# Nine small blank products for one large, and five pieces of work put in another place, in a fused attention and mixer kernel

## The chip, the cores and the metric

The kernel runs on one core of a Trainium2 chip. A core has a matrix engine (TensorE, in the profile PE, with its weight loads as PEld), a vector engine (VectorE, DVE), a scalar engine (ScalarE, ACT), a general engine (GpSimd, POOL) and SyncE (SP), which here only issues transfers. The engines run side by side, each through its own list of instructions in order, and wait for one another through semaphores. Transfers are done by 16 DMA engines; SP, and in this kernel ScalarE too, issue them. The metric is the device time of one execution in microseconds (us).

## The reference

Linear attention with decay by blocks of 64 positions, and then a mixer with a low-rank product and a two-layer part. Shapes: q, k, v are (4, 8, 768, 64), all fp32.

```
per block b of 64 positions, per head:
  intra = ((qb kb^T) * Dmask) vb          # Dmask[i,j] = lam^(i-j) for i >= j
  inter = (qb * lam_pow) kv_state
  out   = intra + inter
  kv_state = lam^64 * kv_state + (kb * rev_pow)^T vb
x = out as (4, 768, 512)
u = x + ((x^T U) V)^T                     # U: 768 x 32, V: 32 x 768
result = u + relu(u w_ch1) w_ch2          # w_ch1: 512 x 2048, w_ch2: 2048 x 512
```

U, V and both weights come as 64-bit floats, so the kernel turns their words into fp32 on VectorE and ScalarE. Products of the mixer are done to near fp32 precision: each operand is split into a high part, a low part and a sum of both, and three products are added up.

## The kernel before, in words

**Attention.** A step s covers 128 positions of one batch; there are 24 steps, six to a batch. The order of all instructions of this stage is written out by hand in the list `pieces` (L698 to L732): the loop over s appends names, and each name is one function. In a step the order around the change is: `prep(s+1)` transposes q and k of the next step on PE and copies them to SBUF on ScalarE; then `intra(s)` multiplies the masked scores `sm` by v into the PSUM tile `px` (L506 to L517), `state(s)` makes the next state kv from k and v (absent in the last step of a batch), `next_v` issues the next load of v from ScalarE, and `inter(s)` multiplies the scaled q by the state and adds that into the same `px` (L519 to L527); then ScalarE copies `px` to `x_nat` (L531). After it come the scores of the next step (`pss`, L463), and VectorE multiplies them by the mask in two halves (`sm`, L472). Up to step 6 `state` stands ahead of `intra`, from step 7 on behind it. `px` has one buffer of two banks, and so have `pss` and `pqk`, the tile for the transposes.

**Start.** While the first loads run, PE multiplies a blank tile with itself (`keep_busy`, L397 to L401): two products, then the tiny product `pl` which spreads lam over the partitions (L830), then three more. The first transposes follow.

**Mixer, first product.** The last steps of attention leave work that runs between the products of the first four pairs (`hidden`, L875 to L906): the list `rest` puts the low-rank part and the transposes (`turn`) of the last steps at given places between the matmuls. Each pair adds up in PSUM banks tagged a1 and a2, two buffers each; ScalarE copies the first (`r`, L896), VectorE adds the second (L905). A transposed step of the last two groups goes through a bank tagged b1, from where ScalarE copies it to the tile `u_whole` (L664). Steps 16 and 17 are turned within the first pair's products.

Then single products (L958, 145 us to 295 us of the profile), and products by seven forms (`seven_of`), which save one product in eight. Between them, `strew` puts side work at the ticks of a counter.

**Mixer, second product.** Each of 96 steps needs a block of the first product's result, fetched from memory (`rm`), its relu and its split into three parts: one ScalarE instruction (L1296) and two on VectorE (L1297, L1298) in `split`. The first two splits are strewn over the last four ticks of the products by forms, where VectorE also adds up the forms' results (`add_to`, L1199), which read the PSUM banks that the next products write. The steps that follow (L1312, L1314, L1316) are laid out in the same loop that fetches and splits ahead.

Of the kernel before, what the change touches and what calls it, by code (L numbers as in the profile page):

```python
# [11 lines left out]
AF = mybir.ActivationFunctionType  # L12
ALU = mybir.AluOpType

P = 128
# [3 lines left out]
def kernel(  # L19
# [28 lines left out]
    nc = tc.nc  # L48

    B, H, S, D = q.shape  # L50
    HP = H // 2
    NT = S // P
# [7 lines left out]
    NS = B * NT  # L60
# [5 lines left out]
    NEAR = 1.0 - 2.0**-13  # L66
# [19 lines left out]
    ends = []  # L86
# [223 lines left out]
    def two_banks(name, tag):  # L310
        return psf.tile([P, 2, N], FP32, tag=tag, name=name)
# [12 lines left out]
    raw = {}  # L324
# [68 lines left out]
    st = {}  # L393
    kv = {}
    half = [slice(0, D), slice(D, P)]

    def keep_busy(n):  # L397

        out = two_banks("idle", "pm")[:, 0]
        for i in range(n):  # L400
            nc.tensor.matmul(out=out[:, 0:P], lhsT=blank, rhs=blank, start=True, stop=True)  # L401

    qts, kts = {}, {}

# [97 lines left out]
    def next_v(s):  # L502
        del raw[s, "v"]
        load_next("v", nc.scalar)

    def intra(s):  # L506

        st[s]["px"] = both = two_banks("px", "px")
        px = both[:, :, 0 : HP * D].rearrange("p x (a e) -> p x a e", a=HP)
        sm, vr, alone = st[s]["sm"], raw[s, "v"], s % NT == 0  # L510
        for x in range(2):
            for a in range(HP):
                for t in range(2):
                    nc.tensor.matmul(  # L514
                        out=px[half[t], x, a, :], lhsT=sm[:, x, a, half[t]],
                        rhs=vr[:, 2 * a + x, :], start=(a == 0), stop=(alone and a == HP - 1),
                    )  # L517

    def inter(s):  # L519

        px = st[s]["px"][:, :, 0 : HP * D].rearrange("p x (a e) -> p x a e", a=HP)
        for a in range(HP if s % NT else 0):
            for x in range(2):
                for t in range(2):
                    nc.tensor.matmul(  # L525
                        out=px[half[t], x, a, :], lhsT=st[s]["qs"][half[x], a, half[t]],
                        rhs=kv[s][half[x], a, :], start=False, stop=(a == HP - 1),  # L527
                    )
        pool, tag = (att, "x10") if s % 10 == 5 else (x_pool, "x")
        xs[s] = pool.tile([P, C], FP32, tag=tag, name="x_nat")  # L530
        nc.scalar.copy(xs[s].rearrange("p (a x e) -> p x a e", a=HP, x=2), px)  # L531
        del st[s]
# [110 lines left out]
    whole, whole_pool = {}, []  # L643

    def store(s):
        nc.sync.dma_start(out=u_d[s], in_=xs[s])

    def turn(s):

        g, n = divmod(s, TG)  # L650
        if n == 0 and g >= FG:
            whole[g] = whole_pool[0].tile([P, CT, N], FP32, tag="u", name="u_whole")
        elif n == 0:
            uhl[g] = hl_pool.tile([P, 2, CT, N], F32R, tag="hl", name="u_hl")
            ud[g] = d_pool.tile([P, CT, N], F32R, tag="d", name="u_d")
        if g >= FG:
            pt = bank([P, CT, P], "put", "b1")
            for ct in range(CT):
                nc.tensor.transpose(
                    out=pt[:, ct, :], in_=xs[s][:, ct * P : (ct + 1) * P], identity=ident  # L660
                )
            store(s)
            del xs[s]
            nc.scalar.copy(whole[g][:, :, n * P : (n + 1) * P], pt)  # L664
            return

        hi, low, diff = (
            by_halves(what)[:, 2 * n : 2 * n + 2].rearrange("p t c i -> p t (c i)")
            for what in (uhl[g][:, 0], uhl[g][:, 1], ud[g])
        )  # L670
        both = both_halves(s + 1)[:, :, 0 : 2 * P]
        pt = both.rearrange("p t (c i) -> p t c i", i=D)
        for ct in range(CT):
            for n in range(2):
                nc.tensor.transpose(
                    out=pt[:, n, ct, :], in_=xs[s][half[n], ct * P : (ct + 1) * P],
                    identity=ident[half[n], half[n]],
                )
# [14 lines left out]

        splits[s] = split
# [4 lines left out]
    for s in range(NS):  # L699
        b, c = divmod(s, NT)  # L700
        done = s - NT - 1
        more = s + 1 < NS
        turns = done > 0 and (done - 1) // TG < FG
        mixes = 0 <= done < NS - NT - 1
        rows = c == 0 and b > 0
        step = [("fade", s)] * (c > 0)
        step += [("mix", done)] * (mixes and c != 1) + [("turn", done - 1)] * turns
        step += [("split", done - 1)] * turns
        step += [("next_of_low", b - 1)] * (s == NT)
        step += [("prep", s + 1)] * more  # L710
        step += [("mix", done + 1)] * (not more)
        step += [("next_of_low", b - 1)] * (rows and s > NT)
        step += [("scale", s + 1)] * more
        step += [("mixed", done)] * (mixes and c != 1)
        step += [("late", s - 1)] * (1 < s < NT - 1 or s > NT)
        step += [("turned", done - 2)] * (done > 1 and c == 1)
        step += [("mixed", done + 1)] * (not more)
        both = [("intra", s), ("state", s)]
        step += (both if s > NT else both[::-1]) + [("next_v", s), ("inter", s)]
        step += [("next_of_low", b - 1)] * rows  # L720
        step += [("late", s)] * (s < 2 or s in (NT - 1, NT))
        step += [("turned", done - 1)] * (done > 0 and c > 0)
# [17 lines left out]
    run = {  # L740
        "prep": prep, "fade": fade, "scores": scores, "masked": masked, "inter": inter,
        "intra": intra, "state": state,
        "low": low, "low_rows": low_rows, "next_of_low": next_of_low, "mix": mix, "turn": turn,
        "mixed": mixed, "store": store, "next_v": next_v, "split": lambda s: splits.pop(s)(),
# [69 lines left out]
    blank = x_pool.tile([P, C], FP32, tag="x", name="blank")[:, 0:P]  # L814
# [13 lines left out]
    pl = two_banks("pl", "pss")[:, 0, 0:H]  # L828
    keep_busy(2)
    nc.tensor.matmul(out=pl, lhsT=lam_row[:, H:], rhs=lam_row[:, 0:H], start=True, stop=True)  # L830
    keep_busy(3)
    nc.vector.tensor_copy(out=lamb, in_=pl)
    constants()
    powers()
# [96 lines left out]
    for i, (pair, ft) in enumerate(head):  # L931
        before = {}
        for unit, n, *piece in rest:
            if unit == i:
                before.setdefault(n, []).append(piece)
        hidden(ft, pair, before)
        for n, step in side:
            if n == i:
                step()
# [219 lines left out]
    for t in range(4, len(stream_steps)):  # L1159
        n = 2 * t - (4 if t == 4 else 5)  # L1160
# [124 lines left out]
    rs, ms = {}, {}  # L1285
# [6 lines left out]
    def split(i):  # L1292
        r = rs.pop(i)
        ms[i] = m = m_pool.tile([P, 3, N], F32R, tag="m", name="m")
        hi, low = m[:, 0].bitcast(FP32), m[:, 1].bitcast(FP32)
        nc.scalar.activation(out=m[:, 0], in_=r, func=AF.Relu, scale=NEAR)  # L1296
        nc.vector.scalar_tensor_tensor(m[:, 1], r, 0.0, hi, ALU.max, ALU.subtract)  # L1297
        nc.vector.scalar_tensor_tensor(m[:, 2], hi, E, low, ALU.mult, ALU.subtract)  # L1298

    us = {}  # L1300
    acc = {}
# [87 lines left out]
    for n in range(3):  # L1389
        strew((total - 9 + n,), [lambda n=n: fetch(n)])  # L1390
    for n in range(2):
        strew((total - 4 + 2 * n,), [lambda n=n: split(n)])
    w2_late = [w2_split(ft) for ft in range(EARLY, FT)]
    for n in range(2):
        strew((total - 2 + n,), w2_late[n][:1])
# [25 lines left out]
    for i in range(FT - EARLY, len(steps) - STAG):  # L1421
        g, ft = steps[i]
# [11 lines left out]
    for n in range(TG):  # L1434
        ends = [slice(0, C // 2), slice(C // 2, C)] if n == TG - 1 else [slice(0, C)]
# [36 lines left out]
```

## Time and profile before

| what | value |
|---|---|
| median of 3 runs (lowest to highest) | 640.4 us (638.09 to 643.14) |
| the profiled execution: its time, its span | 640.24 us, 638.5 us |
| PE busy | 628.4 us, 98% of the span |
| weight loads, VectorE, ScalarE, GpSimd busy | 83%, 73%, 52%, 23% |
| granted TensorE clock over the span | 1.000 |
| share of PE in the chain that ended last | 95% |
| moved by DMA | 129.61 MB, mean 203 GB/s |

The page of the profile gives busy time of each engine. Its chain follows the work back from the last instruction, at each step to whatever released it. A line of the timeline gives the start, the length, the engine, the line of the kernel, what is written from what, the shape, how many records were merged, and in brackets how long the engine had been idle and what ended that; a line of the chain gives start, length and what ran. "issue" is time in which an engine waited for nothing that the profile can name. The ends of matmuls are modelled, so neighbouring ones overlap in the timeline and do not in the chain.

### The profile page before, as it was taken

The page shows a single profiled execution, that of the slowest core. Times are in us where ns is not written, and L with a number is a line of the kernel's source. Part 1 is how long each engine was busy: PE and PEld are TensorE (multiplying, and loading weights), DVE is VectorE, ACT ScalarE, POOL GpSimd, SP SyncE. Part 2 cuts the span into 40 slices and gives each one's busy share as a digit, 9 for nine tenths or more (in the row PEclk, how much of TensorE's full clock was granted, in tenths as well). Part 3 has the DMA queues.
Part 4 walks back from the last instruction along what each step waited for, and adds up shares of the span by engine and source line. Part 5 has one row for each costly group of instructions (what it writes and reads, how often), then busy time and mean ns, then how long its engine had stood idle before and what let it go on. Part 6 is the DMA issues. An engine that isn't in the chain of part 4 may idle for free.

```text
span 638.5 us, 13622 instructions
## 1 busy us (share of the span) xinstructions
PE 628.4 (98%) x5197; PEld 529.0 (83%) x5197; DVE 463.0 (73%) x740; ACT 334.3 (52%) x615; POOL 147.0 (23%) x125
## 2 busy tenths in 40 slices
PE   8899999999999999999999999999999999999997
PEld 7888989888888888888888878888888888888886
DVE  6756778757888788797888799685674755855844
ACT  4675767445777777778777654232322322323220
POOL 4475959100000000000566500030110300300300
PEclk9999999999999999999999999999999999999999
DMA  9979996347798888855776696362363363532521
GB/s 230 244 186 269 233 248 163 135 175 268 260 354 281 280 306 290 292 195 190 250 232 229 227 332 216 112 225 95 113 216 99 127 203 93 190 131 99 182 83 66
DMA packets 141955, 129.61 MB, mean 203 GB/s; under 512 B 82562, under 2 KB 99970, under 8 KB 141890
## 3 DMA queue, kind: packets, MB, share of 16 engines
q1 hardware_dynamic: 116768, 122.32, 59.4%
q10 hardware_dynamic: 25122, 6.42, 4.5%
q8 instruction: 41, 0.67, 0.4%
q14 instruction: 24, 0.20, 0.1%
HBM read 79.04 MB, written 49.28 MB: 201 GB/s over the span
## 4 chain that ended last, share of the span: by engine, by line
PE 95%; ACT 2%; issue 1%; DMA 1%; DVE 1%; DVEq 0%; ACTq 0%
PE pz L958 24%; PE pz L1314 14%; PE pz L1312 14%; PE pd L1316 13%; PE z L958 4%; PE px L514 4%; PE pss L463 4%; PE p L958 3%; PE pz L889 2%; PE d L958 2%; PE px L525 2%; PE pqk L416 2%; PE c L958 2%; PE pkv L486 1%; PE pd L900 1%
## 5 line engine op out<-in xcount | busy, mean ns | idle before, releaser
L1296 ACT ACTIVATE m<-rm 128x512 fp32r<-128x512 f32 x96 | 60.6, 631 | 174.6 <-PE pd L1316 136.6
L1297 DVE SCALAR_TENSOR_TENSOR m<-rm,m 128x512 fp32r<-128x512 f32 x96 | 71.6, 747 | 82.1 <-ACT m L1296 82.1
L958 PE MATMUL pz<-u_hl,w 128*128 128x512 f32 x448 | 110.3, 389 | 0.0
L1312 PE MATMUL pz<-w_hl,m 128*128 128x512 f32 x264 | 102.7, 389 | 0.0
L1314 PE MATMUL pz<-w_hl,m 128*128 128x512 f32 x264 | 102.7, 389 | 0.0
L1316 PE MATMUL pd<-w_d,m 128*128 128x512 f32 (+1 forms) x267 | 101.4, 387 | 0.0
L958 PEld LDWEIGHTS pz<-u_hl,w 128*128 128x128 f32 x448 | 84.1, 188 | 17.4
L285 POOL TENSOR_TENSOR w<-w 128x512 fp32r<-128x512 f32 x29 | 40.5, 1415 | 211.4 <-DVE w L279 197.1
L1298 DVE SCALAR_TENSOR_TENSOR m<-m 128x512 fp32r<-128x512 f32 x96 | 74.9, 780 | 3.1
L1344 POOL TENSOR_TENSOR o<-o,u 128x512 f32<-128x512 f32 x20 | 29.8, 1519 | 199.1 <-DVE o L1340 199.1
L958 PE MATMUL pz<-u_d,w 128*128 128x512 f32 x224 | 59.9, 389 | 0.0
L1316 PEld LDWEIGHTS pd<-w_d,m 128*128 128x128 f32 x267 | 49.9, 188 | 10.3
L1312 PEld LDWEIGHTS pz<-w_hl,m 128*128 128x128 f32 x264 | 49.6, 188 | 10.3
L1314 PEld LDWEIGHTS pz<-w_hl,m 128*128 128x128 f32 x264 | 49.6, 188 | 10.2
L958 PEld LDWEIGHTS pz<-u_d,w 128*128 128x128 f32 x224 | 42.0, 188 | 8.8
L1312 PE MATMUL pz<-w,m 128*128 128x512 f32 x120 | 46.7, 389 | 0.0
L1316 PE MATMUL pd<-w,m 128*128 128x512 f32 x120 | 46.7, 389 | 0.0
L1314 PE MATMUL pz<-w,m 128*128 128x512 f32 x120 | 46.7, 389 | 0.0
L965 ACT ACTIVATE pz<-pz 128x512 f32<-128x512 f32 x56 | 32.5, 581 | 26.4 <-PE pz L958 26.4
L472 DVE TENSOR_TENSOR sm<-pss,mask 128x512 f32<-128x512 f32 x48 | 30.9, 686 | 19.8 <-PE pss L463 19.8
L969 ACT ACTIVATE r<-pz 128x512 f32<-128x512 f32 x56 | 33.2, 595 | 12.0 <-PE pz L958 11.4
L196 DVE SCALAR_TENSOR_TENSOR sc<-words,sc 128x512 uint32<-128x512 uint32 (+2 forms) x34 | 23.8, 700 | 17.6 <-ACT sc L178 17.6
(140 smaller groups left out, 1119.5 us busy)
## 6 DMA issues: line engine op xcount, KB each, us to landing
r_d<-r SPq DMA_DIRECT2D x96, 256.0 KB, 2.9
rm<-r_d SPq DMA_DIRECT2D x96, 256.0 KB, 2.6
words<-in_moe_w_ch_dram SPq DMA_DIRECT2D x30, 512.0 KB, 5.1
wf<-forms_d SPq DMA_DIRECT2D x56, 128.0 KB, 2.9
u_d<-x_nat SPq DMA_DIRECT2D x24, 256.0 KB, 4.2
u<-u_d SPq DMA_DIRECT2D x24, 256.0 KB, 4.5
qraw<-in_q_dram SPq DMA_DIRECT2D x23, 256.0 KB, 4.6
out_dram<-o SPq DMA_DIRECT2D x23, 256.0 KB, 2.0
```

The source lines that it names most:

```text
L285: engine.tensor_tensor(out=st["third"], in0=st["low"].bitcast(FP32), in1=st["hi"].bitcast(FP32), op=ALU.subtract,)
L472: nc.vector.tensor_tensor(out=sm[:, x], in0=pss[:, x], in1=mask[:, x], op=ALU.mult)
L958: nc.tensor.matmul(out=out, lhsT=weights, rhs=moving, start=start and i == 0, stop=i == len(pieces) - 1, skip_group_check=not start,)
L965: nc.scalar.mul(acc, acc, 1.0 + E)
L969: nc.scalar.mul(r, acc, 4096.0)
L1296: nc.scalar.activation(out=m[:, 0], in_=r, func=AF.Relu, scale=NEAR)
L1297: nc.vector.scalar_tensor_tensor(m[:, 1], r, 0.0, hi, ALU.max, ALU.subtract)
L1298: nc.vector.scalar_tensor_tensor(m[:, 2], hi, E, low, ALU.mult, ALU.subtract)
L1312: nc.tensor.matmul(out=pz, lhsT=m[:, 0, cols], rhs=hi, start=first, stop=False)
L1314: nc.tensor.matmul(out=pz, lhsT=m[:, 1, cols], rhs=low, start=False, stop=end)
L1316: nc.tensor.matmul(out=pd[:, part], lhsT=m[:, 2, cols], rhs=third[:, part], start=first, stop=end, skip_group_check=part.stop != C,)
L1344: nc.gpsimd.tensor_tensor(out=o, in0=o, in1=u, op=ALU.add)
```

## The change

Six edits, all of place or number:

1. `keep_busy` makes its first two products of a call with 128 columns and the rest with 16 columns of the blank tile, and the second call makes 11 products instead of 3. So ahead of the first transposes stand two of 128 and nine of 16 columns.
2. In steps 5, 7 and 23 `inter` comes ahead of `intra`, and so the first to write `px`; the flags that start and end the accumulation are set accordingly. The tile is taken by whichever comes first.
3. The ScalarE copy of `px` becomes a function of its own, `take_x`, behind both; in the other steps it stands where it stood.
4. In `turn` of step 17 the ScalarE copy to `u_whole` is put off until all of the first pair's products are issued, so it stands behind that pair's two `r` copies on ScalarE.
5. `split` is cut in two, and the VectorE half of the second split is strewn one tick later. On VectorE its two instructions thereby move behind three of `add_to`'s.
6. With that, one load of `rm` on SP, whose buffer those instructions empty, comes to stand behind a load of u instead of ahead of it.

Apart from these, the order of instructions on each engine is the same.

```diff
         for i in range(n):
-            nc.tensor.matmul(out=out[:, 0:P], lhsT=blank, rhs=blank, start=True, stop=True)
+            k = P if i < 2 else D // 4
+            nc.tensor.matmul(
+                out=out[0:k, 0:k], lhsT=blank[:, 0:k], rhs=blank[:, 0:k], start=True, stop=True
+            )
...
+    inter_first = (NT - 1, NT + 1, NS - 1)
...
+        begins, ends = s not in inter_first, s in inter_first or s % NT == 0
...
-                        rhs=vr[:, 2 * a + x, :], start=(a == 0), stop=(alone and a == HP - 1),
+                        rhs=vr[:, 2 * a + x, :], start=(begins and a == 0),
+                        stop=(ends and a == HP - 1),
...
-                        rhs=kv[s][half[x], a, :], start=False, stop=(a == HP - 1),
+                        rhs=kv[s][half[x], a, :], start=(begins and a == 0),
+                        stop=(not begins and a == HP - 1),
...
+    whole_late = []
...
-            nc.scalar.copy(whole[g][:, :, n * P : (n + 1) * P], pt)
+            take = lambda: nc.scalar.copy(whole[g][:, :, n * P : (n + 1) * P], pt)
+            if s == NS - NT - 1:
+                whole_late.append(take)
+            else:
+                take()
...
-        step += (both if s > NT else both[::-1]) + [("next_v", s), ("inter", s)]
+        if s in inter_first:
+            step += [("inter", s)] + both + [("next_v", s)]
+        else:
+            step += (both if s > NT else both[::-1]) + [("next_v", s), ("inter", s)]
+        step += [("take_x", s)]
...
-    keep_busy(3)
+    keep_busy(3 + 8)
...
         hidden(ft, pair, before)
+        for take in whole_late:
+            take()
+        whole_late.clear()
...
+    def split(i):
+        split_high(i)
+        split_rest(i)
...
-        strew((total - 4 + 2 * n,), [lambda n=n: split(n)])
+        now = total - 4 + 2 * n
+        strew((now, now + n), [lambda n=n: split_high(n), lambda n=n: split_rest(n)])
```

More of the change, by code (lines that the diff above doesn't have):

```diff
@@ L504, in next_v, with px_of @@
         load_next("v", nc.scalar)
+    inter_first = (NT - 1, NT + 1, NS - 1)
+    def px_of(s):
+        if "px" not in st[s]:
+            st[s]["px"] = two_banks("px", "px")
+        return st[s]["px"][:, :, 0 : HP * D].rearrange("p x (a e) -> p x a e", a=HP)
     def intra(s):
-        st[s]["px"] = both = two_banks("px", "px")
-        px = both[:, :, 0 : HP * D].rearrange("p x (a e) -> p x a e", a=HP)
-        sm, vr, alone = st[s]["sm"], raw[s, "v"], s % NT == 0
+        px = px_of(s)
+        sm, vr = st[s]["sm"], raw[s, "v"]
+        begins, ends = s not in inter_first, s in inter_first or s % NT == 0
         for x in range(2):
@@ L515, in intra @@
                         out=px[half[t], x, a, :], lhsT=sm[:, x, a, half[t]],
-                        rhs=vr[:, 2 * a + x, :], start=(a == 0), stop=(alone and a == HP - 1),
+                        rhs=vr[:, 2 * a + x, :], start=(begins and a == 0),
+                        stop=(ends and a == HP - 1),
                     )
     def inter(s):
-        px = st[s]["px"][:, :, 0 : HP * D].rearrange("p x (a e) -> p x a e", a=HP)
+        px, begins = px_of(s), s in inter_first
         for a in range(HP if s % NT else 0):
@@ L526, in inter, with take_x @@
                         out=px[half[t], x, a, :], lhsT=st[s]["qs"][half[x], a, half[t]],
-                        rhs=kv[s][half[x], a, :], start=False, stop=(a == HP - 1),
-                    )
+                        rhs=kv[s][half[x], a, :], start=(begins and a == 0),
+                        stop=(not begins and a == HP - 1),
+                    )
+    def take_x(s):
+        px = px_of(s)
         pool, tag = (att, "x10") if s % 10 == 5 else (x_pool, "x")
@@ L740 @@
     run = {
-        "prep": prep, "fade": fade, "scores": scores, "masked": masked, "inter": inter,
+        "prep": prep, "fade": fade, "scores": scores, "masked": masked, "inter": inter, "take_x": take_x,
         "intra": intra, "state": state,
@@ L1290, in fetch, with split_high, split_rest @@
         nc.sync.dma_start(out=rs[i], in_=r_d[ft][g])
-    def split(i):
-        r = rs.pop(i)
+    def split_high(i):
         ms[i] = m = m_pool.tile([P, 3, N], F32R, tag="m", name="m")
+        nc.scalar.activation(out=m[:, 0], in_=rs[i], func=AF.Relu, scale=NEAR)
+    def split_rest(i):
+        r, m = rs.pop(i), ms[i]
         hi, low = m[:, 0].bitcast(FP32), m[:, 1].bitcast(FP32)
-        nc.scalar.activation(out=m[:, 0], in_=r, func=AF.Relu, scale=NEAR)
         nc.vector.scalar_tensor_tensor(m[:, 1], r, 0.0, hi, ALU.max, ALU.subtract)
         nc.vector.scalar_tensor_tensor(m[:, 2], hi, E, low, ALU.mult, ALU.subtract)
+    def split(i):
+        split_high(i)
+        split_rest(i)
     us = {}
```

## The prediction

> **What bounds the kernel now.** First the page: busy times, then the chain that ended last; then the table by stage, for where TensorE (PE) is not full.
>
> ```profile
> PE 628.4 (98%) x5197; PEld 529.0 (83%) x5197; DVE 463.0 (73%) x740; ACT 334.3 (52%) x615; POOL 147.0 (23%) x125
> ```
> ```profile
> PE 95%; ACT 2%; issue 1%; DMA 1%; DVE 1%; DVEq 0%; ACTq 0%
> ```
> ```profile
> 0.00:115.00 115.00, 108.98 (x2852) 100.14 (x2852) 80.60 (x157) 72.24 (x166) 75.97 (x76) 1.00 0.90 220
> 115.00:145.00 30.00, 30.00 (x198) 24.17 (x191) 18.74 (x36) 15.42 (x29) 0.75 (x1) 1.00 0.46 158
> ```
>
> PE is the bound almost from end to end: 628.4 of 638.5 us busy, 95% of the chain. (Columns of the table: the stretch, its length, then PE, weight loads, VectorE, ScalarE and GpSimd busy, granted clock, DMA share, GB/s.) No useful product is removed, so what the change can win lies in PE's few waits: 115.00 - 108.98 = 6.0 us in the attention stage, and nothing by this count in the 30 us behind it, though short waits show there in the chain. All the edits together therefore move tenths of a microsecond each, and 1% of the time is 6.4 us.
>
> **The change part by part.** *Blank products.* Ahead of the first transposes the second call goes from three products of 128 columns to two of 128 and nine of 16. Each fp32 product is two records.
>
> ```profile
> 2.20 0.59 PE L830 MATMUL pl<-lam_row 1*128 1x8 f32 x2
> 2.73 1.65 PE L401 MATMUL idle<-blank 128*128 128x128 f32 x6
> 5.45 0.29 PEld L416 LDWEIGHTS pqk<-ident,kraw 64*128 64x128 f32 x4 [0.18 <-DMA kraw<-in_k_dram]
> 5.99 2.08 PE L463 MATMUL pss<-qt,kt 64*128 64x128 f32 x16
> 10.22 1.16 PE L463 MATMUL pss<-qt,kt 64*128 64x128 f32 x16
> 11.85 0.46 PE L416 MATMUL pqk<-ident,qraw 64*128 64x64 f32 x8 [0.47 <-DMA qraw<-in_q_dram]
> 16.15 0.46 PE L416 MATMUL pqk<-ident,qraw 64*128 64x64 f32 x8 [0.32 <-DMA qraw<-in_q_dram]
> ```
> ```profile
> 2.80 1.58 PE idle L401 x6
> 60.41 1.45 PE pp L541 x48
> ```
>
> A blank record costs 1.58/6 = 0.263 us here, so the one removed gives back 0.53. The trace has no record of 16 columns. From below: pp's records, with 32-column weights, come every 1.45/48 = 0.030 us at the later, faster pace and four side by side. From above: pl multiplies only 8 columns and still spans 0.59 us for two, about like a blank record, so a cost that did not shrink at all would be 0.263. I take 0.06, twice the lower end because records run about half as fast here (2.08 us for sixteen pss records at 5.99, 1.16 at 10.22). Then 18 x 0.06 - 0.53 = +0.55: the blanks end at 4.9 instead of 4.38 (2.80 + 1.58). The transposes after them wait for k to land anyway (0.18 at 5.45, and as much at 4.77), so perhaps 0.3 of it reaches pss. What hides that: the transposes at 11.85 wait 0.47 for q and those at 16.15 another 0.32, and SP issues these loads one behind another from the start. A start up to 0.3 late, or earlier, only changes these waits. I put the edit at **0.0**. Its bounds: 18 x 0.03 - 0.53 = 0 at the low end; at 0.263 a record +4.20, less some 0.25 hidden at the k waits and 0.47 + 0.32 at the q waits, gives +3.2.
>
> The Trainium skill ("TensorE: Matmul & The Clock Gate", section on LDWEIGHTS) puts the time of a weight load at its number of columns over 1.2 GHz, whatever the rows. By that a 16-column load is an eighth of a 128-column one, an estimate of 0.263/8 = 0.033 us, and the blanks would end within 0.1 us of where they do now; the pl row fits it, since its weights have 128 columns. The sum stays with 0.06.
>
> *State's part of x first, at steps 5, 7 and 23.* The same 32 and 32 records; only their order changes. Before, the scores' part waits for VectorE's mask product, and only then comes the state's part, whose inputs are long there.
>
> ```profile
> 29.75 0.35 issue
> 30.10 1.26 PE px L514 x32
> ```
> ```profile
> 26.61 0.93 PE px L514 x32
> ```
> ```profile
> 29.31 1.29 DVE L472 TENSOR_TENSOR sm<-pss,mask 128x512 f32<-128x512 f32 x2 [2.15 <-PE pss L463]
> 31.39 0.37 ACTq L337 DMA_DIRECT2D vraw<-in_v_dram  x1
> 32.05 0.59 ACT L531 COPY x_nat<-px 128x512 f32<-128x512 f32 x1 [1.13 <-PE px L525]
> 37.33 0.97 PEld L463 LDWEIGHTS pss<-qt,kt 64*128 64x128 f32 x16 [0.28 <-ACT kt L422]
> 41.59 0.50 PE L618 MATMUL pm<-vp 64*128 64x256 f32 x4
> ```
>
> Step 5: before, 0.35 idle and a stretched 1.26 against an undisturbed 0.93 one step earlier: 0.35 + 0.33 = 0.68 us, which the state's 0.62 (row at 41.04 below) now fills (29.75 + 0.62 = 30.37, and VectorE's second half is out at 30.60, when the second half of the products begins). px ends near 31.3 instead of 32.0. But ScalarE now issues v's load (0.37) between the end of the scores' part and its copy of x, where before it did so during the state's part: the copy starts at about 31.3 + 0.05 + 0.37 = 31.7 instead of 32.05. From there to the next pss (37.33, released by ScalarE's kt) the chain runs over ScalarE, so the gain that lasts is 0.33, not 0.68: **-0.33**, between 0 and -0.68.
>
> Step 7: the same is there, 0.35 + (1.24 - 0.93) = 0.66,
>
> ```profile
> 38.98 0.35 issue
> 39.34 1.24 PE px L514 x32
> 40.57 0.47 PE pkv L486 x16
> 41.04 0.62 PE px L525 x32
> ```
> ```profile
> L595 SPq DMA_DIRECT2D vp<-vp x2: 586/901/1216, 37.4 to 38.7; - x2
> ```
> ```profile
> DMA to landing us min/median/max: 3.4/3.4/3.4
> ```
>
> but the products behind it (pm, at 41.59) read rows that SP's four small copies spread, and the last is issued at 38.7 and lands 3.4 later, near 42.1 (rather sooner, as pm starts at 41.59 and shows no wait). With px and state out at 38.98 + 0.62 + 0.93 + 0.47 = 41.0, PE waits there instead: **-0.05**, between 0 and -0.6.
>
> Step 23:
>
> ```profile
> 113.30 1.24 PE px L514 x32
> ```
>
> The stretch is 1.24 - 0.93 = 0.31; the mask's second half is not out much before the scores' part gets to it, so I take **-0.25**, between 0 and -0.31. Behind it stand the 30 us of PE without an idle stretch, so this one lasts.
>
> *The copy of u, behind the first pair's two r copies.*
>
> ```profile
> 122.35 0.59 ACT L664 COPY u_whole<-put 128x512 f32<-128x512 f32 x1
> 122.83 1.09 ACT L896 ACTIVATE r<-pz 128x512 f32<-128x512 f32 x2
> 123.48 0.19 PEld L889 LDWEIGHTS pz<-u_hl,w 128*128 128x128 f32 x1 [0.26 <-ACT r L896]
> ```
> ```profile
> 123.66 0.81 PE pz L889 x2
> 124.71 0.69 PE pz L889 x3
> ```
>
> The second pair's sums use the banks which these r copies empty. The copies would start at 122.35 instead of 122.83, 0.48 sooner, so PE's waits for them go: two products take 2 x 0.23 (0.69/3) = 0.46 of the 0.81, **-0.35**, between -0.2 and -0.4. The u copy itself comes at 123.4; the bank it empties is next needed by the next group of transposes but one, as the pool holds two, several us on, so nothing becomes late.
>
> *The second relu's VectorE half, one tick later.*
>
> ```profile
> 370.72 0.68 DVE L1297 SCALAR_TENSOR_TENSOR m<-rm,m 128x512 fp32r<-128x512 f32 x1
> 371.36 1.14 PE L958 MATMUL z<-s_hl,w 128*128 128x512 f32 x4
> 372.05 0.68 DVE L1199 SCALAR_TENSOR_TENSOR r<-d,r 128x512 f32<-128x512 f32 x1
> 372.65 1.28 DVE L1199 SCALAR_TENSOR_TENSOR r<-p,r 128x512 f32<-128x512 f32 x2
> 372.79 0.73 PE L958 MATMUL d<-s_d,w 128*128 128x512 f32 x2 [0.29 <-DVE r L1199]
> ```
>
> PE's last d products overwrite a bank which VectorE's r<-d at 372.05 still reads, and that one stands behind the m at 370.72 and its second one, which fills the time to 372.05. Put first, it is held only by the ScalarE copy that z at 371.36 waited for too, and is over by about 371.95; PE then goes on when z is through, at 371.36 + 4 x 0.23 = 372.3 instead of 372.79: **-0.4**, between +0.2 and -0.5. What is late next: the m's come behind the two r<-p, at 373.2 to 374.6, needed by the second step's products at about 375.6 (twelve of 0.23 from 372.9): covered by 1 us. The final r<-d slips to about 375.2; the bank it reads is the last that the first step's fourth row block writes, at about 375.4: 0.2 to spare. On SP one load of rm now stands behind one of u and waits for the m's, some 1.7 us later; it is needed four steps on.
>
> Sum: 0.0 - 0.33 - 0.05 - 0.25 - 0.35 - 0.4 = **-1.4 us**. The profiled execution took 640.24 (span 638.5), 0.16 under the median of 640.4, so the forecast is 640.4 - 1.4 = **639.0**. The three runs shown lie 5 us apart (638.09 to 643.14), more than the change.
>
> **Rivals.** (1) *Waits only change their name.* The gains at 5, 7 and 23 go to ScalarE's kt, the spread copies and masks, and the final r<-d catches PE at 375. For: step 7 shows it. Against: from 115 on PE has no other wait to meet. Left is the u copy alone: 640.4 - 0.35 = 640.0.
> (2) *Slower, by the blanks.* If a 16-column record costs nearly what a 128-column one does, as the 8-column pl does, the start is late by more than both q waits hide: +3.2 - 1.4 = +1.8, 642.2. It overturns the rest from 18x - 0.53 - 0.25 - 0.79 = 1.4, x = 0.165 us a record. Against: pl's weights are 128 wide, the blanks' 16.
> (3) *The faster pace comes sooner.* PE has short waits before 4.3 which the blanks fill; were pss at 5.99 at the later pace, 2.08 - 1.16 = 0.9 us, and with the transposes 1.1, would be won ahead of 11.85. If the loads of q came earlier with it, the time is 640.4 - 1.4 - 1.1 = 637.9. Against: the q loads sit in a row of issues on SP that PE does not set off; then PE just waits 1.1 longer at 11.85. The Trainium skill (same page, "Part 1: The HAM clock gate") has such a rule: the array runs at half clock until a window of about 3.4 us was busy, and the window runs freely, so the moment varies from run to run. The granted clock in the table is 1.00 from the start, so only the durations show it.
> (4) *The change doesn't do what it says.* PE has waits that no engine releases:
>
> ```profile
> 25.59 0.40 PE L416 MATMUL pqk<-ident,kraw 64*128 64x64 f32 x7 [0.62 <-issue]
> ```
>
> in the middle of a group of transposes. If the 16 records net that the blanks add shift such pauses onto others, any of the gains can drown in one or two: +-0.6 each, about 640.
>
> **How the numbers follow.** Forecast 0.55; (1) 0.2 and (4) 0.05 near 640; (2) 0.1; (3) 0.1. The cases span 637.9 to 642.2; the spread of runs (a median of few moves by 1 to 2 us) widens that, and the unknown blanks hold the upper end: 636.2 to 642.4. Against the 6.4 us that a measurement of this kernel can tell from nothing, only something none of the rows shows could matter: faster 0.03, same 0.94, slower 0.03.
>
> **What would show it.** After: blank records of 16 columns within 0.1 us each and the first transposes before 5.1; a longer or shorter wait for q near 11.85 with everything behind 16 us where it was; at step 5 the state's part starting right behind the transposes, and pss behind it at about 37.0; at step 7 a wait ahead of pm; no wait on ScalarE's r at the second pair; d without a wait at the end of the products by forms, and everything after it 1.4 earlier in the span. Wrong if the last r<-d holds a product near 375, or if blanks reach beyond 5.5.

## The result, and the profile after

The changed kernel takes **637.88 us** (median of 22 runs, 636.38 to 639.58), the kernel before beside it 640.11 us (22 runs, 638.09 to 643.99). The ratio is 0.9962, with a 95% interval from 0.9949 to 0.9975, or -3.3 to -1.6 us. So the change helps by 0.4%, which is less than the 1% named in the prediction. The forecast was 639.0.

The profiled execution took 637.47 us, with a span of 635.7. The page's lines of busy time and of the chain, and then the table by stage, cut where the first product of the mixer starts (columns as in the prediction):

```profile
PE 628.5 (99%) x5213; PEld 530.3 (83%) x5213; DVE 465.2 (73%) x740; ACT 334.3 (53%) x615; POOL 147.1 (23%) x125
```
```profile
PE 97%; ACT 1%; DMA 1%; DVE 0%; issue 0%; ACTq 0%; DVEq 0%
```
```profile
0.00:113.16 113.16, 109.79 (x2868) 101.43 (x2868) 82.36 (x156) 72.41 (x166) 75.88 (x76) 1.00 0.92 224
113.16:143.16 30.00, 30.00 (x194) 24.53 (x189) 19.34 (x37) 15.29 (x29) 0.96 (x1) 1.00 0.45 158
```

PE's busy time is what it was (628.5 against 628.4). The time that it stood idle in the attention stage went from 6.0 to 113.16 - 109.79 = 3.4 us. The mixer's first product starts 1.86 us earlier (at 113.23 instead of 115.09) and from there to the end the execution takes 0.91 us less (524.24 instead of 525.15). The second of these two numbers comes back in every profile that was taken; the first does not.

**Fourteen profiles side by side.** The experiments below left fourteen profiles of kernels that have all, some or none of the edits. Three numbers of each tell most of what follows. The first is the start of the first `pz` product. The last is the time of the execution less that start, so everything behind it. Between them stands the sum of PE's pauses of more than 0.15 us between 8 us and that start which no engine and no transfer releases and which stand at a block of instructions, as the last section explains. "Copies and relu" are edits 4 and 5; "order" is the state's part first in steps 5, 7 and 23.

| profile | edits in it | time | first `pz` at | pauses | behind it |
|---|---|---|---|---|---|
| before | none | 640.24 | 115.09 | 2.71 | 525.15 |
| e4 | none | 640.85 | 115.68 | 2.14 | 525.17 |
| e13 | none | 640.07 | 114.84 | 0.00 | 525.23 |
| e9 | two large blanks more | 638.26 | 113.10 | 0.59 | 525.16 |
| e1 | small blanks | 640.31 | 115.14 | 2.00 | 525.17 |
| e2 | order | 639.45 | 114.23 | 1.70 | 525.22 |
| e3 | copies and relu | 640.38 | 116.14 | 2.21 | 524.24 |
| e5 | all but the blanks | 638.65 | 114.41 | 1.65 | 524.24 |
| e11 | all but the blanks | 640.69 | 116.45 | 4.03 | 524.24 |
| after | all | 637.47 | 113.23 | 0.71 | 524.24 |
| e10 | all | 636.78 | 112.51 | 0.23 | 524.27 |
| e8 | all, copy of x sooner | 638.69 | 114.46 | 1.71 | 524.23 |
| e12 | all, copy of x sooner | 638.48 | 114.22 | 1.55 | 524.26 |
| e6 | all, 32 small blanks more | 643.19 | 118.91 | 2.81 | 524.28 |

The last column has two values and nothing between: 525.15 to 525.23 without the u copy and the relu edit, 524.23 to 524.28 with them, a gain of 0.93 us by the means. All that differs from one execution of a kernel to the next lies ahead of the first `pz`, in a range of some 4 us.

### The profile page after: what moved, and what is told of

Its sections match the earlier page's. It is cut to its first block, busy times and chain, and to the rows that moved or that the text cites. A ratio compares the mean times of both kernels' runs of the same rounds, so it can differ in the third digit from the quotient of the medians.

```text
span 635.7 us, 13659 instructions
## 1 busy us (share of the span) xinstructions
PE 628.5 (99%) x5213; PEld 530.3 (83%) x5213; DVE 465.2 (73%) x740; ACT 334.3 (53%) x615; POOL 147.1 (23%) x125
## 3 DMA queue, kind: packets, MB, share of 16 engines
q10 hardware_dynamic: 25122, 6.42, 4.5%
## 4 chain that ended last, share of the span: by engine, by line
PE 97%; ACT 1%; DMA 1%; DVE 0%; issue 0%; ACTq 0%; DVEq 0%
PE pz L986 24%; PE pz L1346 14%; PE pz L1348 14%; PE pd L1350 14%; PE z L986 5%; PE px L524 4%; PE pss L466 4%; PE p L986 3%; PE pz L914 2%; PE d L986 2%; PE px L536 2%; PE pqk L419 2%; PE c L986 2%; PE pkv L489 2%; PE pd L925 1%; PE pm L633 1%
## 5 line engine op out<-in xcount | busy, mean ns | idle before, releaser
L1350 PEld LDWEIGHTS pd<-w_d,m 128*128 128x128 f32 x267 | 49.8, 188 | 10.2
L1346 PEld LDWEIGHTS pz<-w_hl,m 128*128 128x128 f32 x264 | 49.5, 188 | 10.2
```

The source lines that it names most:

```text
L1346: nc.tensor.matmul(out=pz, lhsT=m[:, 0, cols], rhs=hi, start=first, stop=False)
L1350: nc.tensor.matmul(out=pd[:, part], lhsT=m[:, 2, cols], rhs=third[:, part], start=first, stop=end, skip_group_check=part.stop != C,)
```

## The experiments

Four runs of edits apart share one chip and its runs of the kernel before (642.05 us, 29 runs, 639.27 to 647.07).

**e1: the blanks alone**, added to the kernel before.

```diff
+            k = P if i < 2 else D // 4
...
-    keep_busy(3)
+    keep_busy(3 + 8)
```

> The kernel before with the blank products of after alone (two of 128 and nine of 16 columns). Sum of parts (as predicted): a start up to 0.3 us late is swallowed by the waits for q near 11.85 and 16.15, so 0.0 us against before, between -0.3 and +0.3. Rival, pauses: the 16 added records move the places at which PE pauses without a releaser, and the pauses at 20.38, 25.59 and 63.59 of before (0.5 to 0.8 us each) go, as they have gone in the profile of after: -1.3 to -2 us. Rival, pace: the blanks bring the faster pace of PE forward: the first sixteen pss records take about 1.2 us instead of 2.1.

Measured: 640.31 us (12 runs), ratio 0.9964 (0.9941 to 0.9987). By itself this looks like a gain of 2.3 us. But of the 29 runs of the kernel before beside these four 13 have a mean granted clock of 0.993 to 0.997 and a median of 644.35; the other 16 have 640.48, and none of e1's 12 show such a clock. Against 640.48, e1 is 0.2 us lower, and its profile is as long as that of the kernel before (640.31 and 640.24). As work on the path the blanks are worth nothing that these runs can show.

**e2: the order of steps 5, 7 and 23 alone**, added to the kernel before.

```diff
+    inter_first = (NT - 1, NT + 1, NS - 1)
```

> The kernel before with the state's part of x first at steps 5, 7 and 23 alone. Sum of parts: as predicted -0.63 us (0.33, 0.05, 0.25); read from the two traces, step 5 gives nothing lasting, step 7 0.1 and step 23 0.2, so -0.3. Pauses: no records are added, so the same -0.3 to -0.6, with the pauses of before still there.

Measured: 641.54 us (12 runs), ratio 0.9984 (0.9958 to 1.001). The three places can be read one by one from the starts of `pss` in all profiles; that is done in the next section, and step 5 turns out to give nothing.

**e3: the copy of u and the relu alone**, added to the kernel before.

```diff
+            if s == NS - NT - 1:
+                whole_late.append(take)
...
+        strew((now, now + n), [lambda n=n: split_high(n), lambda n=n: split_rest(n)])
```

> The kernel before with the later copy of u and the later VectorE half of the second relu alone. Sum of parts: -0.75 us as predicted, -0.37 - 0.58 = -0.95 by the two traces. Pauses: the attention stage is the same program as before, so the same -0.95, and nothing more.

Measured: 640.29 us (12 runs), ratio 0.9975 (0.9947 to 1.0003). Its interval holds the expected and holds zero. The profile settles it: behind the first `pz` it takes 524.24, exactly what the changed kernel takes.

**e4: the kernel before once more** (no edit), for a second profile of it.

> The kernel before once more, for a second profile. If the pauses without a releaser belong to the program, they stand again near 20.4, 25.6, 35.1 and 63.6 us and the time at which the first product of the mixer begins is 115.2 within 0.3. If they belong to the execution, they stand elsewhere, and that time differs by about 1 us.

Measured: 640.85 us. It starts the mixer at 115.68 and takes 525.17 behind it, within 0.02 of the first profile. Of the seven pauses of the first profile ahead of the mixer three stand here again, at the same instructions (58.70, 64.32 and 87.88 us), with other lengths: 0.49, 0.79 and 0.86 us where the first had 0.21, 0.78 and 0.18. The other four are gone.

The next four share another chip (kernel before: 639.62 us, 35 runs, 638.12 to 645.13).

**e5: all but the blanks**, which are those of the kernel before.

```diff
-            k = P if i < 2 else D // 4
...
-    keep_busy(3 + 8)
+    keep_busy(3)
```

> The kernel after with the three large blank products of before. Theory, spells of a lower clock: without the added blanks a quarter to a half of its runs again have a mean granted clock below 0.9985 and are 2 to 5 us longer (before beside it likewise); among the runs at the full clock its median is 1.2 us below that of before, which is what the other edits took from the marks in the profiles (0.25 by the order, 0.95 by the copy and the relu). Rival, sum of parts alone: no such runs, and the median is that of after. Rival, pauses without a releaser belong to the blanks: those near 20.4, 25.6 and 63.6 stand in its profile, 1 to 2 us of them more than in after's.

Measured: 638.89 us (12 runs), ratio 0.9989 (0.997 to 1.0009). That is less of a gain than the whole change had beside its own runs of the kernel before. It was tried again beside the changed kernel as e11, below, where both were the same.

**e6: forty products more instead of eight**, in the changed kernel.

```diff
-    keep_busy(3 + 8)
+    keep_busy(3 + 40)
```

> The kernel after with 41 products of 16 columns in place of 9, so 64 records more, at 0.031 us as the weight loads of after show, 2.0 us. Theory of the prediction: the waits for k and q at the start swallow some 1 us of it, so the products behind 28 us stand about 1 us later than in after, and the time is +1.0 us against after. Rival, the start is fully covered: 0. Rival, nothing is covered: +2.0. No runs with a mean clock below 0.9985, if blanks are what keeps them away.

Measured: 643.0 us (10 runs), ratio 1.0045 (1.0026 to 1.0063), so +2.9 us against the kernel before. Expected was +1.0 against the changed kernel, which did not run on this chip; e5 and e8 beside it, which differ from it little, took 638.89 and 638.56, so e6 is some 4 us above it, four times what was expected. The weight loads of the blanks in the timeline, of the changed kernel and of e6:

```profile
2.72 0.93 PEld L402 LDWEIGHTS idle<-blank 128*128 128x128 f32 x4
3.87 0.56 PEld L402 LDWEIGHTS idle<-blank 128*16 128x16 f32 x18 [0.22 <-issue]
5.85 0.48 PE L419 MATMUL pqk<-ident,kraw 64*128 64x64 f32 x4 [0.27 <-DMA kraw<-in_k_dram]
6.12 2.18 PE L466 MATMUL pss<-qt,kt 64*128 64x128 f32 x16
```
```profile
3.87 2.26 PEld L402 LDWEIGHTS idle<-blank 128*16 128x16 f32 x82 [0.22 <-issue]
7.61 1.66 PE L466 MATMUL pss<-qt,kt 64*128 64x128 f32 x12 [0.31 <-ACT kt L425]
```

A record of 16 columns takes 0.56/18 = 0.031 us, and 2.26/82 = 0.028 in the longer row. The 64 more records put the first scores at 7.61 instead of 6.12, 1.49 us later, and at step 9 it is 1.55 (46.92 against 45.37): the waits for q, which were to swallow 0.8 of it, don't occur in this execution, nor in any other profile with small blanks. Up to the first `pz` another 4 us are lost. Its pauses from there on explain 1.8 of them (2.49 against 0.71), and two waits for the spread copies, which the changed kernel's profile doesn't have, another 0.94:

```profile
71.09 0.47 PE L633 MATMUL pm<-vp 64*128 64x256 f32 x3 [0.63 <-DMA vp<-vp]
102.05 0.47 PE L633 MATMUL pm<-vp 64*128 64x256 f32 x3 [0.31 <-DMA vp<-vp]
```

What the last 1.4 us are was not found, and one profile doesn't tell how much of all this another execution of e6 would show.

**e8: the copy of x ahead of v's load**, in steps 5, 7 and 23 of the changed kernel.

```diff
-            step += [("inter", s)] + both + [("next_v", s)]
+            step += [("inter", s)] + both + [("take_x", s), ("next_v", s)]
```

> The kernel after with ScalarE's copy of x ahead of the issue of v's load at steps 5, 7 and 23. From pss of step 6 to pss of step 7 before takes 5.42 us and after 5.95; if the issue of 0.38 between px and its copy is the cause, it is 5.6 here, and the time 0.3 us below after; if the late vt on VectorE is the cause, it stays 5.9.

Measured: 638.56 us (12 runs), ratio 0.9977 (0.9957 to 0.9997), 0.3 us under e5 and not to be told from it.

**e9: two large blanks more**, ahead of the first transposes of the kernel before, all of 128 columns.

```diff
-    keep_busy(3)
+    keep_busy(5)
```

> The kernel before with five blank products of 128 columns in the second call instead of three: four records more at 0.263, 1.05 us. If filling PE up to the first transposes keeps the lower clock away, no run has a mean clock below 0.9985, and the median falls by 1 to 2 us although the start is late by up to 1 us, of which the q waits swallow most. If it takes the many small records, a quarter to a half of the runs have the lower clock, as in before, and the median is that of before or up to 0.5 above.

Measured: 639.78 us (12 runs), ratio 1.0001 (0.9979 to 1.0023). Four large records, 4 x 0.263 = 1.05 us of blanks by the row of the kernel before, cost nothing that these runs can tell (the interval is -1.3 to +1.5 us). In its profile the first scores start 0.6 later (6.59 against 5.99) and the second at 10.22 as before: here the start is hidden, unlike in e6.

The last four share a third chip (kernel before: 640.16 us, 29 runs, 637.13 to 643.2).

**e10: the changed kernel again** (no edit), **e11: without the blanks** (the edit of e5), **e12: the copy of x ahead of v's load** (the edit of e8), **e13: the kernel before** (no edit).

> The kernel after, beside the same without the added blanks, to be compared on one chip. Theory, spells of a lower clock: no run with a mean clock below 0.9985, or one; its median is 1.0 to 1.4 us below that of before's runs at the full clock, and further below that of all of before's runs the more of them have the lower clock. Sum of parts alone: 1.2 us below before whatever the clocks.

> The kernel after with the three large blanks of before, once more. Theory, spells of a lower clock: a sixth to a half of the runs have a mean clock below 0.9985, and those are 2 to 4 us longer; its runs at the full clock are those of after within 0.3 us. Rival, the blanks shorten the start itself: the runs at the full clock are 0.5 to 1 us above those of after.

> The kernel after with ScalarE's copy of x ahead of the issue of v's load at steps 5, 7 and 23, beside after on one chip. From pss of step 5 to pss of step 7: 9.0 us as in its first profile, against 9.3 to 9.5 with the issue ahead (after, and after with forty more blanks); the time 0.3 us below after, which is within what these rounds can tell.

> The kernel before, a third profile. If its mean clock is below 0.9985, the slices show where the lower clock lies: in the attention stage (0 to 115 us), if it hangs on the waits of the start, or anywhere, if it does not. At the full clock it gives one more set of pauses without a releaser: those of the second profile (58.7, 64.3 and 97 us) stand again, if they belong to the program.

Measured: e10 638.04 us (ratio 0.9968, 0.995 to 0.9987), e11 638.25 (0.9975, 0.9959 to 0.9992), e12 637.95 (0.9968, 0.9954 to 0.9983), 12 runs each; e13 640.07, one run. The three are one and the same within 0.3 us. With the blanks or without, and with the copy of x on either side of v's load, the kernel is 2 us faster than before.

## Why the prediction was right, and which of its steps failed

**The copy of u: right, -0.37 for -0.35.** The chain at the second pair, of e2 (which leaves the copy where it was) and of the changed kernel:

```profile
122.81 0.82 PE pz L911 x2
```
```profile
121.80 0.45 PE pz L914 x2
```

The two products that waited for ScalarE's r now take 0.45 us, two times 0.23.

**The relu's half: right in its mechanism, larger than said, -0.56 for -0.4.** The gain of 0.93 behind the first `pz` less the 0.37 above. The timeline of the changed kernel at the end of the products by forms:

```profile
369.03 0.69 DVE L1227 SCALAR_TENSOR_TENSOR r<-d,r 128x512 f32<-128x512 f32 x1 [0.46 <-ACT r L1231]
370.08 0.62 PE L986 MATMUL d<-s_d,w 128*128 128x512 f32 x2
370.84 0.68 DVE L1327 SCALAR_TENSOR_TENSOR m<-rm,m 128x512 fp32r<-128x512 f32 x1
372.16 0.68 DVE L1227 SCALAR_TENSOR_TENSOR r<-d,r 128x512 f32<-128x512 f32 x1
372.60 0.39 PE L1346 MATMUL pz<-w,m 128*128 128x512 f32 x1
```

r<-d stands ahead of the m's, and d has no wait and is 0.62 long instead of 0.73. The prediction counted the gap (372.79 - 372.3 = 0.49, taken as 0.4) and not the 0.11 by which the waiting d was stretched; the two make 0.60. What it held to be late next is not: the last r<-d starts at 372.16, which is 374.97 on the clock of the kernel before (this stage runs 2.81 us earlier now), where 375.2 was said, and neither the fourth row block (372.60) nor a product of the second step waits.

**Step 23: right, -0.21 for -0.25, though from a wrong length.** From the scores of step 23 to the first `pz` it is 3.78 to 3.79 us in the profiles of the old order and 3.56 to 3.58 in those of the new. The chain of the changed kernel:

```profile
111.59 0.62 PE px L536 x32
112.22 1.08 PE px L524 x32
113.30 1.81 PE pz L914 x7
```

The scores' part takes 1.08, not the 0.93 that the prediction used as its undisturbed length at all three steps. That 0.93 was a misreading: in the chain the row of step 4 begins only where the modelled end of the products before it lies. The timeline of the kernel before has the same 32 records, with no wait ahead of them:

```profile
26.44 1.10 PE L514 MATMUL px<-vraw,sm 128*64 128x64 f32 x32
```

In the chain of the kernel before, too, step 22 takes 1.10 (from 109.12). The stretch at step 23 is therefore 1.24 - 1.10 = 0.14 and not 0.31, and with an idle 0.06 ahead of it, which the prediction didn't count, 0.20. That -0.25 came near is in part luck.

**Step 7: -0.16 for -0.05, and another wait than the one named.** From the scores of step 7 to those of step 9 it is 8.96 to 9.05 us in the old order (six profiles) and 8.79 to 8.87 in the new (eight). The prediction had PE wait for the spread copies at the first `pm`. The timeline of PE in the changed kernel:

```profile
39.76 0.64 PE L489 MATMUL pkv<-vraw,ks 128*64 128x64 f32 x16
40.33 0.50 PE L633 MATMUL pm<-vp 64*128 64x256 f32 x4
40.67 1.05 PE L466 MATMUL pss<-qt,kt 64*128 64x128 f32 x16
41.96 0.50 PE L633 MATMUL pm<-vp 64*128 64x256 f32 x4 [0.24 <-DVE x_nat L645]
```

The first `pm` starts at 40.33, straight behind `pkv`: the copies had landed, so their 3.4 us from issue to landing was no bound. The wait comes one piece later, at the second `pm`: the tile has one buffer, and VectorE's sum into `x_nat` (L645) must first have read it. The chain says why that is late:

```profile
40.45 0.46 DVE kv L500 x2
40.91 0.12 issue
41.03 0.27 DVE kv L500
41.30 0.61 DVE x_nat L645
```

VectorE first makes the next state, which waits for `pkv`, and only then `x_nat`. With the length of 1.08 that the scores' part has here (chain, at 38.85), the edit could win 0.35 + (1.24 - 1.08) = 0.51 and not 0.66. Of this 0.24 turned into that wait (0.23 or 0.24 in all eight profiles of the new order), as rival (1) had it, with another engine; 0.16 is left, and 0.1 is not accounted for.

**Step 5: the step that failed, nothing for -0.33.** From the scores of step 5 to those of step 7, profiles with a pause at a block of instructions in between left out: 9.21 to 9.51 us in the old order (e4, e9 and e13), 9.29 to 9.52 in the new (after, e6 and e10). With three profiles of each and ranges of 0.2 to 0.3 us, a gain as large as forecast would show, one of 0.1 would not. The prediction's chain was: px ends 0.7 sooner, v's load takes 0.37 of it on ScalarE, the copy of x and everything behind it gains 0.33. From the timeline of PE in the kernel before, and from the timeline of PE and the chain of the changed kernel:

```profile
28.10 1.16 PE L463 MATMUL pss<-qt,kt 64*128 64x128 f32 x16
31.91 1.16 PE L463 MATMUL pss<-qt,kt 64*128 64x128 f32 x16
```
```profile
27.00 1.16 PE L466 MATMUL pss<-qt,kt 64*128 64x128 f32 x16
30.57 1.16 PE L466 MATMUL pss<-qt,kt 64*128 64x128 f32 x16
```
```profile
28.94 0.62 PE px L536 x32
29.56 1.11 PE px L524 x32
30.67 0.02 issue
30.69 0.38 ACTq L337
31.06 0.04 issue
31.11 0.59 ACT x_nat L546
```

The load costs what was said (30.69 to 31.11, 0.42). But the next scores, which follow px, start 30.57 - 27.00 = 3.57 us behind those of step 5, where it was 31.91 - 28.10 = 3.81 before: PE gained 0.24, not 0.7. Two terms were wrong. The scores' part takes 1.11 us on the chain and not 0.93, the misread length. With 1.10 in its place the prediction's own chain puts the copy of x at 29.75 + 0.62 + 1.10 + 0.42 = 31.89 instead of 32.05, a gain of 0.16 and not 0.33. And the state's part begins 28.94 - 27.00 = 1.94 behind the scores, not the 29.75 - 28.10 = 1.65 at which PE's wait began, since the transposes ahead of it are longer in this profile; that takes the 0.16 and more. (By the timeline it is 1.87 here and 1.77 in e10, and 1.58 to 1.59 in the other profiles of the new order, so this second term is one of the execution.) With 0.24 gained and 0.42 paid, the copy of x starts 31.11 - 27.00 = 4.11 behind the scores (4.00 in e10) against 32.05 - 28.10 = 3.95. ScalarE's casts follow it, and its kt releases the scores of step 7, no sooner than before.

e8 and e12 put the copy ahead of v's load, and ScalarE does start it sooner: 3.40 and 3.42 after the scores of step 5. What stands behind it, in the timelines of ScalarE of e8 and e12:

```profile
31.91 0.58 ACT L546 COPY x_nat<-px 128x512 f32<-128x512 f32 x1 [0.59 <-PE px L524]
32.71 2.08 ACT L796 CAST vp<-vt 32x384 fp32r<-32x384 f32 x4 [0.21 <-DVE vt L789]
```
```profile
30.32 0.59 ACT L546 COPY x_nat<-px 128x512 f32<-128x512 f32 x1 [0.58 <-PE px L524]
31.75 2.08 ACT L796 CAST vp<-vt 32x384 fp32r<-32x384 f32 x4 [0.85 <-DVE vt L789]
```

Now the casts wait for VectorE's `vt`, by 0.21 in the one and 0.85 in the other, and the step comes to 9.00 and 9.66 (the latter with a pause of 0.18). 9.00 would be a gain of 0.2 or more and 9.66 is none, and it hangs on when `vt` comes. So behind the load there is a second bound, VectorE, which the prediction didn't look for.

**The blanks: right, 0.0, with a cheaper record than said.** 0.031 us a record against the 0.06 that was taken; the sum by it is 18 x 0.031 - 0.53 = 0.03. The estimate of 0.033 from the rule on weight loads in the Trainium skill ("TensorE: Matmul & The Clock Gate", section on LDWEIGHTS) agrees with the 0.031 of the trace, and the lower bound, from the pp row, was nearer than the chosen value. The first transposes start at 4.47 (5.1 was the limit). Rival (2) needed 0.165 a record and is out. The cover that was named, the waits for q, is there in some executions alone: in six of the eight profiles without small blanks, and in none of the six with them. Where PE has no wait for q it reaches the second scores later by itself (11.2 to 12.3 us, against 10.2 to 11.1), and both kinds are at the scores of step 4 by 23.1 to 24.4 (e6 apart, with 12.9 and 25.0). So for the change the cover made no difference; for e6, which needed it, it was missing.

The two kinds differ in when PE's faster pace begins. The traces have a record of the full granted clock, and it begins at 6.42 to 9.99 us in the six executions that wait for q, and at 10.68 to 12.36 in the eight that don't; the clock column counts the time before it as full, which is why it reads 1.00. All six with small blanks are among the late ones and two of the eight others; whether the blanks make it late was not tried apart.

Rival (3), the faster pace sooner, is out as well: the sixteen `pss` records at 6.12 take 2.18 us, no less than before (2.08 at 5.99), and the record of the full clock begins at 11.22 us in the changed kernel and at 8.36 in the kernel before. The first scores' part, before and after, shows the later start:

```profile
9.19 1.10 PE L514 MATMUL px<-vraw,sm 128*64 128x64 f32 x32
```
```profile
9.98 1.67 PE L524 MATMUL px<-vraw,sm 128*64 128x64 f32 x32
```

The moment differs between executions of one kernel, too: 8.36, 9.78 and 9.99 us in the kernel before, 10.68 and 11.22 in the changed one.

**The sum.** By the stretches that can be compared: 0 for the blanks, 0 for step 5, -0.16, -0.21, -0.37 and -0.56 make **-1.3 us**, against -1.4 said: the errors of steps 5 and 7 and of the relu cancel. Measured were -2.2 (interval -3.3 to -1.6) in the first comparison, then -2.1 on the third chip of the experiments (e10, -3.2 to -0.8), and -0.7 without blanks on the second (e5, -1.9 to +0.6). The -1.3 lies in the two later intervals and just outside the first. What is more than 1.3 lies ahead of the first `pz`, by the last column of the table, and no edit was found to own it. (How many of the 22 runs of the kernel before in the first comparison had the lower granted clock of the last section is not on record, so its share can't be told.) The six starts of `pz` in the old order have a mean of 115.0, the seven of the new (without e6) 114.2, with 3 to 4 us between the earliest and the latest of either. Rival (4) was given 0.05 as a case of its own; its mechanism runs in every case, and a pair of profiles says little about the attention stage because of it: of the 2.8 us between the two profiled executions 2.0 is pauses (2.71 against 0.71).

## What to carry to other kernels

Before crediting the difference between two profiles to an edit, cut both at marks that the same work reaches, and compare the stretches over several executions: the stretch behind the mark repeated to 0.08 us here, the one ahead of it only to 4 us. When a wait is taken off an engine, walk the chain on to the second and third engine behind it: step 5 lost its gain to a DMA issue on ScalarE's list and then to VectorE, step 7 to VectorE. A stretched matmul is part of the wait that it stands behind, and counts with it; take the undisturbed length to compare with from the timeline, since a chain's row can begin where the group before it ends (0.93 against 1.10 us here).

## What the runs showed of the hardware that was not expected

**PE pauses where its list enters a new block of 256 records, when the block came late.** The prediction's rival (4) named pauses that nothing releases. Three from the timeline of PE in e11, two in e6, and one in the kernel before:

```profile
20.96 0.49 PE L463 MATMUL pss<-qt,kt 64*128 64x128 f32 x4 [0.42 <-issue]
26.45 0.41 PE L416 MATMUL pqk<-ident,kraw 64*128 64x64 f32 x7 [0.91 <-issue]
89.04 0.38 PE L533 MATMUL px<-kv,qs 64*64 64x64 f32 x9 [1.44 <-issue]
```
```profile
23.58 0.63 PE L524 MATMUL px<-vraw,sm 128*64 128x64 f32 x15 [0.32 <-issue]
82.89 0.50 PE L633 MATMUL pm<-vp 64*128 64x256 f32 x3 [1.54 <-issue]
```
```profile
64.37 0.74 PE L514 MATMUL px<-vraw,sm 128*64 128x64 f32 x18 [0.78 <-issue]
```

Of the 45 counted below 44 stand in the middle of a group of matmuls. Number the records of PE in a trace from 0 in order of start, the products, the weight loads and the semaphore instructions between them: the first three are 706, 961 and 4290, the next two 961 and 4034, the last 3010. Divided by 256, these leave 194, 193, 194, 193, 194 and 194. It is so for all 45 pauses of more than 0.15 us of this kind behind 8 us in the fourteen profiles, of 0.16 to 1.54 us, in kernels whose traces have from 10,512 to 10,677 records of PE: the place in the program moves with the list, the remainder doesn't. The 18 other pauses without a named releaser stand at three fixed places of the program (px of steps 5 and 7, one `pkv` at 94 to 100 us), with any remainder and with 0.28 to 0.35 us each time, so they are ordinary waits without a name in the profile. The page of every one of these kernels has a queue of its own for instructions:

```profile
q8 instruction: 41, 0.67, 0.4%
```

(In e1 the share is 0.5%.) Each of its packets is 16 KB, and there are 41 in every kernel; the records of PE with remainder 193, at which a block is taken to begin, are as many, from 193 to 10,433. The packets' own times in the traces show what PE waits for. All 45 pauses end 1.25 to 1.64 us after the end of the latest packet, and it is the same packet each time, the first packet ahead of record 449, the second ahead of 705, and so on: in the kernel before, packets end at 57.45 and 62.99 us, and the pauses that follow them at 58.75 and 64.37. Of the 250 entries into a block that show no pause between the first packet and the first `pz`, none comes sooner than 1.22 us after its packet. So PE goes on some 1.3 us after its block has come, and pauses when it gets there earlier. This is read from times; no run changed the blocks or their transfers.

All 45 lie ahead of the first `pz`, and none behind it. Ahead of it PE uses up a block in some 4.7 us (4.3 to 5.9 in the kernel before), and the packet for the next ends 1.2 to 5.0 us after PE has entered the one before; from 165 us on a block lasts 28 to 30 us. The DMA engines are busier ahead of it too (0.92 in the changed kernel, against 0.45 in the 30 us behind it), and what that adds was not separated. In one execution these pauses make between 0 and 4.03 us, in the kernel before alone 0, 2.14 and 2.71.

**Some executions have a lower mean granted clock, and kernels with the small blanks hardly had it here.** In the experiments on the three chips and the runs of the changed kernel, 29 of 153 runs without small blanks have a mean granted clock of 0.993 to 0.997 and take some 2 to 5 us longer (0.003 of 638 us is 1.9 us, 0.007 is 4.5); with small blanks it is 1 of 80. Most of them are from the first of these chips (13 of 29 of the kernel before, 7 of 24 in e2 and e3, none of 12 in e1). Without that chip it is 9 of 100 against 1 of 68, which is little to go by. e9's two large blanks don't keep them away (3 of 12). No profiled execution had such a clock, so where in the run it falls, and whether the blanks are the cause, stays open.
